# Banded attention and a gated feed-forward on one core: the planned engine order comes from four forward and backward passes instead of one

## The chip, the core and the metric

The kernel runs on one core of a Trainium2 chip. The metric is the device time of one execution in microseconds (us). The engines are named as the profile names them: PE multiplies matrices, DVE and ACT work on vectors, POOL does a little setup, and SP issues the transfers (DMA). Each engine works through its own queue of instructions in the order in which the program put them there.

## The reference, cut to what matters

```python
# q, k, v: 8 batches x 8 heads x 576 positions x 64, float32
scores = q @ k.T / sqrt(64)                     # per batch and head
mask = (rel >= 0) & (rel < 64)                  # each position sees itself and 63 before it
attn = softmax(where(mask, scores, -1e9))
x = (attn @ v), heads side by side              # 4608 tokens x 512
h = x @ w_in                                    # 512 x 2048
g = (a0 + a1*h + a2*h**2 + a3*h**3) / (1 + |b0|*|h| + |b1|*h**2 + 1e-6)
out = g @ w_out                                 # 2048 x 512, float32
```

## The kernel before, in words

**Tiles.** The 4608 tokens are cut into 12 chunks of 384 (`CH`), the 2048 hidden columns into 16 blocks of 128 (`NF`). A chunk takes four attention units (two heads each, `HP` = 4) and then 16 steps; a step is one hidden block of one chunk, so that there are 192 steps. All large products are made from split operands: each float32 operand is a high part and a low part (`xh`, `xl`; `wi_h`, `wi_l`; `gh`, `gl`; `wo_h`, `wo_l`), and three products are added up.

**A step.** `ffn1` is 12 matmuls into one of two PSUM buffers `h` (4 pieces of x, three products each). `gate` then works the rational function out: ACT squares `h`, takes |b0 h| and a3 h + a2, later a logarithm and an exponential (the division); DVE makes the rest with a multiplication by `h` and a second product with `h` (after which that buffer is free again), the denominator, `gh` and, three instructions later, `gl`. Steps 0 to 3 and the last four are gated alone, all others in pairs with tiles of 768 columns. `ffn2` is 9 matmuls into the three PSUM buffers `o` (three token tiles, three products each) and is recorded three steps after its `ffn1` (`LAG`). In the text, h8 is the `ffn1` of step 8, o8 its `ffn2`, gl 8/9 the last DVE instruction of the gate of steps 8 and 9. As two buffers `h` alternate, h8 waits for the second product with `h` of step 6.

**An attention unit.** Scores into `ps_s` (for the first three chunks the mask is put in by two matmuls from `ident_b`), the row maximum `nmx` on DVE, six exponentials on ACT with row sums `sums`, the scaling of `sm` by `rs` on DVE, transposes on PE into `ps_s`, a copy by ACT, the products with v into `ps_x`, and from these `xh` (ACT) and `xl` (DVE).

**Weights.** The 32 weight pieces come as raw 64-bit words through three staging buffers `w_st` (the first six through spare space). Each is turned into its two parts by two ACT instructions (a cast into `top`, a cast into `wi_h` or `wo_h`) and two DVE instructions (a shift, called the weight shift below, and a subtraction that gives `wi_l` or `wo_l`). The subtraction frees the staging buffer for the next fetch, which SP issues in a fixed order. The steps run in the order chunk 0 and chunk 1 with the first eight hidden blocks, then chunk 1 and chunk 0 with the other eight, then each further chunk with all 16, so that the weights are needed during steps 0 to 23.

**What sets the order.** The body of the kernel issues nothing itself. Its calls go to a `Recorder` (lines 236 to 241), which hands each to a `Planner` (line 54). That keeps them as operations with an occupancy and a latency from hand-set costs (`cost`, line 113), and works out from the tiles that they read and write which operation must follow which (`add`, line 165). `plan` (line 189) then lays all operations out on a time line of its own: again and again it takes the engine that could start next, and on that engine, among the operations that are ready, the one that was recorded first (`key=lambda o: o.index`). PE prefers one that has been ready for 300 ns (`MARGIN`). `fill` (line 217) puts warm-up matmuls into gaps that the plan leaves on PE before the first `ffn2`, and `emit` (line 229) issues everything by planned start. All instructions issued so carry the helper's line, 233 in the profile, and are told apart by their tiles. The hardware keeps each queue's order, and waits are for semaphores: an instruction that waits holds up all behind it on its engine.

Of the kernel before, what the change touches and what calls it, by code (L numbers as in the profile page):

```python
# [30 lines left out]
WARM = 7  # L31
FILL = 430
MARGIN = dict(PE=300)
C1AT = 0, 0, 1, 3
ON_PE = 2
JOIN = 4
# [17 lines left out]
class Planner:  # L54
# [58 lines left out]
    def cost(self, engine, method, out, reads, kw, args):  # L113
        if isinstance(out, Late):
            n = out.size // 4
        else:
            n = 1
            for _, k in out.ap[1:]:
                n *= k
        if engine == "SP":  # L120
            parts = 128 if isinstance(out, Late) else (out.ap[0][1] if out.tensor.__class__.__name__ != "DRamTensorHandle" else 0)
            size = mybir.dt.size(out.dtype) * n * (parts or out.ap[0][1])
            return 400, 400, size
        if engine == "PE":
            if method == "transpose":
                return 109, 270, 0
            if isinstance(args[2], Late):
                n = args[2].size // 4
            else:
                n = 1  # L130
                for _, k in args[2].ap[1:]:
                    n *= k
                if args[2].dtype == F32:
                    return (45, 270, 0) if args[1].ap[0][1] == 64 else (52, 225, 0)
            return n * 0.4545, n * 0.4545 + 165, 0
        if engine == "ACT":
            if "accum_out" in kw:
                return (343, 450, 0) if reads[0].tensor.name in self.banks else (386, 490, 0)
            f = args[2] if len(args) > 2 else None
            occ = 58 + 0.813 * n  # L140
            if n == 512:
                occ = 640 if method == "copy" and getattr(out, "dtype", None) == F16 else 510
                if reads[0].tensor.name in self.banks:
                    occ = 466
            for k in ("scale", "bias"):
                if isinstance(kw.get(k), bass.AP):
                    occ += 92
            if f in (AF.Ln, AF.Exp):
                occ += 55
            return occ, occ + 120, 0  # L150
        if engine == "DVE":
            if method == "tensor_reduce":
                n = 1
                for _, k in reads[0].ap[1:]:
                    n *= k
            if n < 16:
                return 90, 185, 0
            occ = 65 + 1.045 * n
            if isinstance(kw.get("scalar"), bass.AP):
                occ += 62  # L160
            return occ, occ + 85, 0
        if engine == "POOL":
            return (n * 2.0 + 60, n * 2.0 + 100, 0) if method in ("tensor_scalar", "tensor_copy") else (n * 2.4 + 130, n * 2.4 + 170, 0)

    def add(self, op):
        op.index, op.before, op.after = len(self.ops), set(), []
        op.ready = max([self.known.get(name, 0) for name, *_ in op.reads + op.writes], default=0)
        for is_write, spans in ((False, op.reads), (True, op.writes)):
            for name, p0, p1, b0, b1 in spans:
                for q0, q1, c0, c1, other, wrote in self.hist.get(name, ()):  # L170
                    apart = self.ops[other].engine != op.engine
                    if name in self.banks and apart or (wrote or is_write) and p0 < q1 and q0 < p1 and b0 < c1 and c0 < b1:
                        op.before.add(other)
        if op.engine == "SP":
            op.before.update(self.loads[-1:] + self.loads[-self.DMA_LANES:1 - self.DMA_LANES])
            self.loads.append(op.index)
        for other in op.before:
            self.ops[other].after.append(op)
        self.ops.append(op)
        for wrote, spans in ((False, op.reads), (True, op.writes)):  # L180
            for name, p0, p1, b0, b1 in spans:
                h = self.hist.setdefault(name, [])
                if wrote and name not in self.banks:
                    h[:] = [x for x in h if not (p0 <= x[0] and x[1] <= p1 and b0 <= x[2] and x[3] <= b1)]
                h.append((p0, p1, b0, b1, op.index, wrote))
                if name in self.shares:
                    self.hist.setdefault(self.shares[name], []).append((0, 128, 0, 1 << 20, op.index, False))

    def plan(self):
        waiting = {e: [] for e in self.free}  # L190
        missing = [len(o.before) for o in self.ops]
        for o in self.ops:
            if not o.before:
                waiting[o.engine].append(o)
        dma_free = 0
        for _ in self.ops:
            start, engine = min((max(self.free[e], min(o.ready for o in w)), e) for e, w in waiting.items() if w)
            able = [o for o in waiting[engine] if o.ready <= start]
            op = min([o for o in able if o.ready <= start - MARGIN.get(engine, 0)] or able, key=lambda o: o.index)
            waiting[engine].remove(op)  # L200
            op.start, self.free[engine] = start, start + op.occ
            op.end = start + op.own + 45
            if engine == "PE":
                op.end = self.free[engine] + 200
            if engine == "SP":
                dma_free = max(dma_free, start + 750) + op.dma / (300 if start < 8000 else 390)
                op.end = dma_free + 1550
            for o in op.after:
                o.ready = max(o.ready, self.free[engine] if engine == o.engine == "SP" and self.lanes_apart(op, o) else op.end)
                missing[o.index] -= 1  # L210
                if not missing[o.index]:
                    waiting[o.engine].append(o)

    def lanes_apart(self, op, other):
        return self.loads.index(other.index) - self.loads.index(op.index) == 1

    def fill(self, engine, name, length, call):

# [49 lines left out]
def swa_rational_ffn(ctx: ExitStack, tc: tile.TileContext, qk, v, w_in, w_out, out):  # L268
# [371 lines left out]
    for c, i0, i1 in phases:  # L640
        if c not in seen:
            seen.add(c)
            places += [(C1AT[k] if c == 1 else s - prev + prev // HP * k - AHEAD, c, k, s - prev if c > 1 else 0) for k in range(HP)]
        prev = i1 - i0
# [89 lines left out]
```

## Time and profile before

| | |
|---|---|
| time, median of 3 runs | 973.5 us (972.23 to 974.33) |
| the profiled execution's own time | 973.52 us |
| its span, first to last instruction | 971.7 us |
| PE busy | 948.9 us, 98% of the span |
| DVE busy | 856.8 us, 88% |
| ACT busy | 665.9 us, 69% |
| mean granted clock of PE | 0.995 |
| moved by DMA | 68.33 MB, 70 GB/s |

The profile is one execution. A row of its time line gives the start, the duration, the engine and the instruction with its output and inputs; in square brackets stands how long the engine sat idle before it, and what ended that. A row of its table of stages gives for each engine the busy time in that stage, then the granted clock of PE as a share of full speed. Busy times of PE are modelled at their ends: a matmul of the step is shown with 0.33 or 0.39 us, but the next one starts 0.17 or 0.23 us after it.

### The profile page before, as it was taken

The numbers are of one execution on the slowest core, as the hardware profiler recorded it, in microseconds if no ns is written. First come the engines' busy times: TensorE is split into PE (matmuls) and PEld (weight loads), VectorE is DVE, ScalarE is ACT, GpSimd is POOL, SyncE is SP. The second block draws the span as 40 slices with busy tenths as digits, with TensorE's granted clock in tenths as the row PEclk, the third lists the DMA queues.
The fourth block names the chain that finished last, engine by engine and source line by source line (L and its number), as shares of the span: only waits on it lengthen the run. The fifth ranks groups of instructions, "written<-read, shape, count | busy, mean of one in ns | idle before, by whom it ended". The sixth has DMA issues, their size and how long they took to land.

```text
span 971.7 us, 16840 instructions
## 1 busy us (share of the span) xinstructions
PE 948.9 (98%) x6673; PEld 829.1 (85%) x6673; DVE 856.8 (88%) x1287; ACT 665.9 (69%) x1553; POOL 4.4 (0%) x20
## 2 busy tenths in 40 slices
PE   8879999999999999999999999999999999999998
PEld 5667888888888888888888888888888888888896
DVE  6999998888998889888988898998889988997887
ACT  7997876766667667667666667667766766675653
POOL 1000000000000000000000000000000000000000
PEclk9998999999999999999999999999999999999999
DMA  9363431223102113112111210220211211200000
GB/s 358 117 212 109 144 128 56 80 68 101 48 22 101 35 35 101 35 35 95 41 35 67 69 35 34 68 69 12 90 35 36 101 35 36 101 1 1 33 1 32
DMA packets 24558, 68.33 MB, mean 70 GB/s; under 512 B 2720, under 2 KB 2720, under 8 KB 24480
## 3 DMA queue, kind: packets, MB, share of 16 engines
q1 hardware_dynamic: 24480, 67.27, 20.2%
q8 instruction: 52, 0.85, 0.4%
q14 instruction: 26, 0.21, 0.1%
HBM read 57.03 MB, written 10.22 MB: 69 GB/s over the span
## 4 chain that ended last, share of the span: by engine, by line
PE 88%; DVE 8%; ACT 3%; issue 1%; DMA 1%; SPq 0%; ACTq 0%; DVEq 0%
PE o L233 40%; PE h L233 38%; PE ps_s L233 6%; PE ps_x L233 4%; DVE tmp L233 3%; ACT tmp L233 1%; DVE gh L233 1%; DMA early_wi_h<-w_in 1%; DVE w_st L233 1%; DVE wi_l L233 1%; DVE gl L233 0%; DVE sm L233 0%; ACT sm L233 0%; DVE nmx L233 0%; DVE wo_l L233 0%
## 5 line engine op out<-in xcount | busy, mean ns | idle before, releaser
L233 PE MATMUL h<-xl,wi_h 128*128 128x384 f32 x768 | 260.2, 339 | 5.1 <-DVE tmp L233 4.3
L233 PE MATMUL h<-xh,wi_l 128*128 128x384 f32 x768 | 259.0, 337 | 0.0
L233 PE MATMUL h<-xh,wi_h 128*128 128x384 f32 x768 | 257.8, 336 | 0.0
L233 ACT ACTIVATE tmp<-h 128x384 f32<-128x384 f32 x192 | 94.3, 491 | 233.1 <-PE h L233 232.8
L233 PE MATMUL o<-wo_h,gl 128*128 128x512 f32 x576 | 236.4, 411 | 3.3 <-DVE gl L233 2.9
L233 PE MATMUL o<-wo_h,gh 128*128 128x512 f32 x576 | 227.7, 395 | 0.0
L233 PE MATMUL o<-wo_l,gh 128*128 128x512 f32 x576 | 227.5, 395 | 0.0
L233 ACT ACTIVATE tmp<-h,ab_sb 128x384 f32<-128x384 f32 x384 | 221.0, 629 | 2.4 <-PE h L233 2.4
L233 ACT ACTIVATE tmp<-tmp 128x768 f32<-128x768 f32 (+1 forms) x200 | 164.6, 823 | 20.6 <-DVE tmp L233 17.8
L233 PEld LDWEIGHTS h<-xl,wi_h 128*128 128x128 f32 x768 | 144.2, 188 | 16.7 <-DVE tmp L233 6.8
L233 PEld LDWEIGHTS h<-xh,wi_h 128*128 128x128 f32 x768 | 144.2, 188 | 7.4
L233 DVE SCALAR_TENSOR_TENSOR gh<-tmp,ab_sb,tmp 128x768 fp32r<-128x768 f32 (+1 forms) x100 | 98.2, 982 | 54.4 <-ACT tmp L233 54.0
L233 PEld LDWEIGHTS h<-xh,wi_l 128*128 128x128 f32 x768 | 144.1, 188 | 0.0
L233 PEld LDWEIGHTS o<-wo_h,gl 128*128 128x128 f32 x576 | 108.3, 188 | 29.0 <-issue 6.4
L233 PEld LDWEIGHTS o<-wo_h,gh 128*128 128x128 f32 x576 | 108.5, 188 | 26.6
L233 PEld LDWEIGHTS o<-wo_l,gh 128*128 128x128 f32 x576 | 108.6, 189 | 16.6
L233 DVE SCALAR_TENSOR_TENSOR tmp<-tmp,ab_sb,h 128x384 f32<-128x384 f32 x192 | 116.9, 610 | 3.0
L233 DVE SCALAR_TENSOR_TENSOR tmp<-tmp,b_sb,tmp 128x768 f32<-128x768 f32 (+1 forms) x96 | 95.8, 998 | 23.9 <-ACT tmp L233 23.8
L233 DVE TENSOR_TENSOR tmp<-tmp,h 128x384 f32<-128x384 f32 x192 | 105.1, 548 | 5.6 <-ACT tmp L233 5.4
L233 DVE SCALAR_TENSOR_TENSOR tmp<-tmp,ab_sb,tmp 128x768 f32<-128x768 f32 (+1 forms) x96 | 95.8, 998 | 1.3
L233 DVE SCALAR_TENSOR_TENSOR tmp<-tmp,gh 128x768 f32<-128x768 f32 (+1 forms) x100 | 92.1, 921 | 1.5
L233 DVE TENSOR_TENSOR gl<-tmp,tmp 128x768 fp32r<-128x768 f32 (+1 forms) x96 | 90.0, 937 | 1.5
(97 smaller groups left out, 784.4 us busy)
## 6 DMA issues: line engine op xcount, KB each, us to landing
qk<-qk SPq DMA_DIRECT2D x42, 419.0 KB, 3.3
vt<-v SPq DMA_DIRECT2D x44, 384.0 KB, 4.0
out<-ob SPq DMA_DIRECT2D x33, 256.0 KB, 2.2
w_st<-w_out SPq DMA_DIRECT2D x15, 512.0 KB, 3.7
w_st<-w_in SPq DMA_DIRECT2D x11, 512.0 KB, 3.9
early<-qk SPq DMA_DIRECT2D x6, 419.0 KB, 8.0
early<-v SPq DMA_DIRECT2D x4, 384.0 KB, 8.5
early_wi_l<-w_in SPq DMA_DIRECT2D x3, 512.0 KB, 9.4
```

Of the source, the lines that this page charges most:

```text
L233: call(*[value(x) for x in args], **{k: value(x) for k, x in kw.items()})
```

## The change

**What it does.** `plan` lays the operations out `ROUNDS` = 4 times instead of once. A round is `forward(rank)`, the old loop with one difference: among ready operations it takes the one of lowest rank. In the first round the rank is the place in the recording, as before. After each round `backward` goes through the operations from the end: it takes them in the order of their ends in the forward pass just made, keeps to the same engines, occupancies and lags, and so finds for each the time, counted back from the end, by which it must have started. Those latest times rank the next round. Of the four layouts that whose last operation ends first (by the planner's own clock) is kept. Beside this, `lag` gives one rule for the time from an operation's start to that of one that depends on it: on PE itself it is now only the occupancy (before, 200 ns more). And the cost of the large matmuls is set from n columns as 0.467 n - 6 ns instead of 0.4545 n, 0.3 ns more at 512 columns and 1.2 ns less at 384.

Nothing in the list of operations changes, nor do tiles, waits or SP's order; what changes is where an operation stands in its engine's queue, and how many warm-up matmuls `fill` adds: 30 with the seven at the start instead of 25.

```diff
+ROUNDS = 4
...
-            if isinstance(args[2], Late):
-                n = args[2].size // 4
-            else:
-                n = 1
-                for _, k in args[2].ap[1:]:
-                    n *= k
+            n = 1
+            for _, k in (args[0] if isinstance(args[2], Late) else args[2]).ap[1:]:
+                n *= k
+            if not isinstance(args[2], Late):
                 if args[2].dtype == F32:
                     return (45, 270, 0) if args[1].ap[0][1] == 64 else (52, 225, 0)
-            return n * 0.4545, n * 0.4545 + 165, 0
+            return n * 0.467 - 6, n * 0.467 + 160, 0
...
     def plan(self):
+        free, best = dict(self.free), None
+        rank = [o.index for o in self.ops]
+        for _ in range(ROUNDS):
+            self.free = dict(free)
+            length = self.forward(rank)
+            if best is None or length < best[0]:
+                best = length, [(o.start, o.end) for o in self.ops]
+            rank = self.backward()
+        for o, (o.start, o.end) in zip(self.ops, best[1]):
+            pass
+
+    def lag(self, op, other):
+        if op.engine == other.engine and (op.engine == "PE" or op.engine == "SP" and self.lanes_apart(op, other)):
+            return op.occ
+        return op.end - op.start
+
+    def forward(self, rank):
...
-            op = min([o for o in able if o.ready <= start - MARGIN.get(engine, 0)] or able, key=lambda o: o.index)
+            op = min([o for o in able if ready[o.index] <= start - MARGIN.get(engine, 0)] or able, key=lambda o: rank[o.index])
...
-                o.ready = max(o.ready, self.free[engine] if engine == o.engine == "SP" and self.lanes_apart(op, o) else op.end)
+                ready[o.index] = max(ready[o.index], start + self.lag(op, o))
...
+        return max(o.end for o in self.ops)
+
+    def backward(self):
+        waiting = {e: [] for e in self.free}
+        missing = [len(o.after) for o in self.ops]
+        free, ready, late = dict.fromkeys(self.free, 0), [0] * len(self.ops), [0] * len(self.ops)
+        for o in self.ops:
+            if not o.after:
+                waiting[o.engine].append(o)
+        for _ in self.ops:
+            time, engine = min((max(free[e], min(ready[o.index] for o in w)), e) for e, w in waiting.items() if w)
+            op = max((o for o in waiting[engine] if ready[o.index] <= time), key=lambda o: (o.start + o.occ, -o.index))
+            waiting[engine].remove(op)
+            late[op.index] = free[engine] = time + op.occ
+            for k in op.before:
+                o = self.ops[k]
+                ready[k] = max(ready[k], late[op.index] + self.lag(o, op) - o.occ)
+                missing[k] -= 1
+                if not missing[k]:
+                    waiting[o.engine].append(o)
+        return [-x for x in late]
```

**Where the order moves.** On PE the two orders differ in the first 920 of some 4300 rows (to about 225 us of the time line before) and in the last six; between them they are the same. On ACT and DVE small exchanges go on to the end. Three places follow, each of before and then of the change; line 233 of the kernel before is line 276 of the changed one.

First PE at about 67 us of the time line before, between the end of o3 (`o_74<-wo_h_136,gh_183`) and o4 (`gl_184`), where `ps_s<-ident` are a unit's transposes and `h_75<-xl_154` begins h8:

```order
L233 MATMUL o_74<-wo_h_136,gh_183 128x512
L233 MATMUL ps_s<-ident,sm_169 128x128 x6
L233 MATMUL o_72<-wo_h_136,gl_184 128x512
L233 MATMUL o_72<-wo_l_137,gh_182 128x512
L233 MATMUL o_72<-wo_h_136,gh_182 128x512
```

```order
L276 MATMUL o_74<-wo_h_136,gh_183 128x512
L276 MATMUL h_75<-xl_154,wi_h_134 128x384
L276 MATMUL h_75<-xh_150,wi_h_134 128x384
L276 MATMUL h_75<-xh_150,wi_l_135 128x384
L276 MATMUL h_75<-xl_155,wi_h_134 128x384
L276 MATMUL h_75<-xh_151,wi_h_134 128x384
L276 MATMUL h_75<-xh_151,wi_l_135 128x384
L276 MATMUL h_75<-xl_156,wi_h_134 128x384
L276 MATMUL h_75<-xh_152,wi_h_134 128x384
L276 MATMUL h_75<-xh_152,wi_l_135 128x384
L276 MATMUL o_72<-wo_h_136,gl_184 128x512
```

Nine of h8's twelve matmuls now stand ahead of the wait for gl 4/5; the transposes have gone behind six of o4's matmuls.

Then DVE at the same time, from the end of step 3's gate (`gl_185<-tmp_181`). The `w_st` rows are weight shifts and subtractions, `b_sb` marks the denominator of steps 4 and 5, and `tmp_179<-tmp_179,ab_sb,h_75` is the second product of step 6, which frees `h_75` for h8:

```order
L233 TENSOR_TENSOR gl_185<-tmp_181 128x384
L233 TENSOR_TENSOR wo_l_137<-w_st_164,wo_h_136 128x512
L233 TENSOR_TENSOR xl_156<-ps_x,xh_152 128x384
L233 SCALAR_TENSOR_TENSOR tmp_177<-tmp_177,b_sb,tmp_178 128x768
L233 SCALAR_TENSOR_TENSOR w_st_165<-w_st_165,top_138 128x512
L233 SCALAR_TENSOR_TENSOR w_st_163<-w_st_163,top_139 128x512
L233 TENSOR_REDUCE nmx_171<-ps_s 128x6
L233 TENSOR_TENSOR wo_l_137<-w_st_165,wo_h_136 128x512
L233 TENSOR_SCALAR nmx_171<-nmx_171 128x6
L233 SCALAR_TENSOR_TENSOR gh_182<-tmp_176,ab_sb,tmp_178 128x768
L233 TENSOR_TENSOR wo_l_137<-w_st_163,wo_h_136 128x512
```

```order
L276 TENSOR_TENSOR gl_185<-tmp_181 128x384
L276 SCALAR_TENSOR_TENSOR tmp_177<-tmp_177,b_sb,tmp_178 128x768
L276 TENSOR_TENSOR wo_l_137<-w_st_164,wo_h_136 128x512
L276 SCALAR_TENSOR_TENSOR w_st_165<-w_st_165,top_138 128x512
L276 TENSOR_TENSOR tmp_179<-tmp_179,h_75 128x384
L276 TENSOR_TENSOR xl_156<-ps_x,xh_152 128x384
L276 SCALAR_TENSOR_TENSOR tmp_179<-tmp_179,ab_sb,h_75 128x384
L276 SCALAR_TENSOR_TENSOR w_st_163<-w_st_163,top_139 128x512
L276 TENSOR_REDUCE nmx_171<-ps_s 128x6
L276 SCALAR_TENSOR_TENSOR gh_182<-tmp_176,ab_sb,tmp_178 128x768
```

The two products of step 6 and the denominator have moved up, weight work has moved down; the second product of step 6 stood 21 rows behind gl 3 and now stands six behind it.

Last PE's end, the final products of step 191 in the three buffers `o`:

```order
L233 MATMUL o_73<-wo_h_1005,gh_183 128x512
L233 MATMUL o_74<-wo_l_1032,gh_183 128x512
L233 MATMUL o_74<-wo_h_1005,gh_183 128x512
L233 MATMUL o_72<-wo_h_1005,gl_185 128x512
L233 MATMUL o_73<-wo_h_1005,gl_185 128x512
L233 MATMUL o_74<-wo_h_1005,gl_185 128x512
```

```order
L276 MATMUL o_73<-wo_h_1087,gh_183 128x512
L276 MATMUL o_72<-wo_h_1087,gl_185 128x512
L276 MATMUL o_74<-wo_l_1132,gh_183 128x512
L276 MATMUL o_74<-wo_h_1087,gh_183 128x512
L276 MATMUL o_73<-wo_h_1087,gl_185 128x512
L276 MATMUL o_74<-wo_h_1087,gl_185 128x512
```

The last matmul into the first buffer `o` has moved up by two.

More of the change, by code (lines that the diff above doesn't have):

```diff
@@ L166, in add @@
         op.index, op.before, op.after = len(self.ops), set(), []
-        op.ready = max([self.known.get(name, 0) for name, *_ in op.reads + op.writes], default=0)
+        op.known = max([self.known.get(name, 0) for name, *_ in op.reads + op.writes], default=0)
         for is_write, spans in ((False, op.reads), (True, op.writes)):
@@ L175, in add @@
             op.before.update(self.loads[-1:] + self.loads[-self.DMA_LANES:1 - self.DMA_LANES])
+            op.turn = len(self.loads)
             self.loads.append(op.index)
@@ L189, in plan @@
     def plan(self):
+        free, best = dict(self.free), None
[13 more added lines that the diff above has]
+    def forward(self, rank):
         waiting = {e: [] for e in self.free}
         missing = [len(o.before) for o in self.ops]
+        ready = [o.known for o in self.ops]
         for o in self.ops:
@@ L196, in plan @@
         for _ in self.ops:
-            start, engine = min((max(self.free[e], min(o.ready for o in w)), e) for e, w in waiting.items() if w)
-            able = [o for o in waiting[engine] if o.ready <= start]
-            op = min([o for o in able if o.ready <= start - MARGIN.get(engine, 0)] or able, key=lambda o: o.index)
+            start, engine = min((max(self.free[e], min(ready[o.index] for o in w)), e) for e, w in waiting.items() if w)
+            able = [o for o in waiting[engine] if ready[o.index] <= start]
+            op = min([o for o in able if ready[o.index] <= start - MARGIN.get(engine, 0)] or able, key=lambda o: rank[o.index])
             waiting[engine].remove(op)
@@ L212, in plan @@
                     waiting[o.engine].append(o)
+        return max(o.end for o in self.ops)
[18 more added lines that the diff above has]
+        return [-x for x in late]
     def lanes_apart(self, op, other):
-        return self.loads.index(other.index) - self.loads.index(op.index) == 1
+        return other.turn - op.turn == 1
     def fill(self, engine, name, length, call):
```

## The prediction

> **What bounds the kernel now.** The profiled execution took 973.52 us, which is the median of the three runs; 971.7 us is its span and 1.8 us lie outside it. I read the chain of work first, then a table of the span cut into stages.
>
> ```profile
> PE 88%; DVE 8%; ACT 3%; issue 1%; DMA 1%; SPq 0%; ACTq 0%; DVEq 0%
> ```
>
> ```profile
> core 0: us, PE busy (x) PEld busy (x) DVE busy (x) ACT busy (x) POOL busy (x), PEclk, DMA share, GB/s
> 20.00:67.00 47.00, 40.98 (x384) 32.71 (x384) 45.71 (x88) 44.70 (x112) 0.00 (x0) 1.00 0.53 183
> 67.00:73.00 6.00, 0.58 (x3) 0.47 (x3) 6.00 (x10) 5.57 (x20) 0.00 (x0) 0.88 0.63 188
> 73.00:79.00 6.00, 6.00 (x39) 4.72 (x38) 4.12 (x8) 2.19 (x4) 0.00 (x0) 0.55 0.20 76
> 79.00:123.00 44.00, 41.75 (x206) 36.28 (x205) 43.02 (x63) 36.06 (x64) 0.00 (x0) 1.00 0.40 138
> 150.00:225.00 75.00, 73.88 (x578) 63.64 (x578) 65.74 (x101) 51.34 (x132) 0.00 (x0) 1.00 0.23 76
> 225.00:944.00 719.00, 719.00 (x5020) 638.52 (x5020) 633.24 (x916) 480.76 (x1105) 0.00 (x0) 1.00 0.15 50
> ```
>
> The chain is PE's for 88%, and from 225 to 944 us PE is never idle at a full clock: no order of the same matmuls shortens that. What an order can win lies elsewhere. Until 123 us DVE is full (45.71 of 47, 6.00 of 6, 43.02 of 44 us) and PE isn't: the weights are split there, and DVE does their shifts and subtractions beside the gates. So I looked next at the time line of PE for the waits in that part.
>
> ```profile
> 66.75 0.40 PE L233 MATMUL o<-wo_h,gh 128*128 128x512 f32 x1
> ...
> 72.56 1.51 PE L233 MATMUL ps_s<-ident,sm 128*128 128x128 f32 x6 [5.42 <-DVE sm L233]
> ...
> 86.44 0.50 PE L233 MATMUL o<-wo_h,gl 128*128 128x512 f32 x1 [0.62 <-DVE gl L233]
> 96.05 0.47 PE L233 MATMUL o<-wo_h,gl 128*128 128x512 f32 x1 [0.96 <-DVE gl L233]
> 122.64 0.44 PE L233 MATMUL h<-xl,wi_h 128*128 128x384 f32 x1 [0.66 <-DVE tmp L233]
> 122.91 0.34 PE L233 MATMUL h<-xh,wi_h 128*128 128x384 f32 x1
> 123.09 0.34 PE L233 MATMUL h<-xh,wi_l 128*128 128x384 f32 x1
> ```
>
> Each wait ends on a DVE instruction, and from 25 to 150 us DVE has no pause of over 0.35 us but one, shown below. What bounds this part is therefore the amount of DVE work that stands in DVE's queue ahead of what PE needs. This is what the new order changes. The long wait has a second cost:
>
> ```profile
> 71.00:72.00 1.00, 0.00 (x0) 0.00 (x0) 1.00 (x2) 1.00 (x3) 0.00 (x0) 0.79 0.26 102
> ```
>
> ```profile
> 78.68 0.56 DVE L233 TENSOR_TENSOR xl<-ps_x,xh 128x384 fp32r<-128x384 f32 x1 [1.88 <-ACT xh L233]
> ```
>
> The granted clock of 0.79 in microsecond 71 means that it fell to one half at about 71.6, some 4.45 us after the last matmul (66.75 + 0.40); in the stage from 73 to 79 us it is 0.55 still. The slow transposes and products then leave DVE idle for 1.88 us, the one real gap in its work of this part.
>
> **What the change does to DVE's queue.** The amount of work is the same; I counted in both orders what stands ahead of each DVE result that PE waits for. The prices are distances from one start to the next:
>
> ```profile
> 81.61 0.69 DVE L233 TENSOR_TENSOR wi_l<-w_st,wi_h 128x512 fp32r<-128x512 f32 x1
> 82.22 0.95 DVE L233 SCALAR_TENSOR_TENSOR tmp<-tmp,gh 128x768 f32<-128x768 f32 x1
> 83.08 0.69 DVE L233 SCALAR_TENSOR_TENSOR w_st<-w_st,top 128x512 uint32<-128x512 uint32 x1
> ```
>
> A weight shift or subtraction costs 0.61 us (82.22 - 81.61), an instruction on 768 columns 0.86 to 0.95 (83.08 - 82.22, and its duration; I take 0.9); for one on 384 columns I take half a microsecond, a little over half of that. Ahead of the second product that frees the buffer for h18 five weight instructions and one on 768 columns have gone: 5 x 0.61 + 0.9 = 3.9 us less. Ahead of gl 18/19 it is four weight instructions less and one on 768 columns more: 1.5 us less. Ahead of gl 20/21 three weight instructions less, two on 384 columns more: 0.8 less. Ahead of gl 8/9 three less, and three gate instructions more: 0.1 more. Ahead of gl 6/7 it is 1.1 less, and ahead of gl 4/5 only 0.2.
>
> A result that comes earlier helps only as far as PE waited for it, and PE's own order moves too. How far PE may get ahead by each point is the margin there, plus DVE work gone, plus PE work that now stands ahead, plus the later waits of the part that PE then no longer has:
>
> ```profile
> 140.40 0.95 DVE L233 TENSOR_TENSOR gl<-tmp,tmp 128x768 fp32r<-128x768 f32 x1
> 147.96 0.96 DVE L233 TENSOR_TENSOR gl<-tmp,tmp 128x768 fp32r<-128x768 f32 x1
> ```
>
> ```profile
> 142.81 0.39 PE L233 MATMUL o<-wo_h,gl 128*128 128x512 f32 x1
> ...
> 149.11 0.42 PE L233 MATMUL o<-wo_h,gl 128*128 128x512 f32 x1
> ```
>
> At o18 gl 18/19 was ready 1.46 us early (142.81 - 141.35); with 1.5 less that allows 2.9. At o20 the margin was 0.19; with 0.8 less, and a whole h (12 matmuls, about 2.0 us) newly ahead of o20, 3.0. At o8 the matmuls placed ahead bring 2.0, and the wait of 0.66 at h18 goes: 2.7 less 0.1. At o6, 1.1 gained, and 0.96 and 0.66 that come later: 2.7. I take **-2.7 us** by about 150 us; what is late next is gl 8/9.
>
> **The wait at o4.** Nine of h8's matmuls now stand between o3 and the wait.
>
> ```profile
> 72.33 0.95 DVE L233 TENSOR_TENSOR gl<-tmp,tmp 128x768 fp32r<-128x768 f32 x1
> ```
>
> The second product of step 6, for which h8 waits, stood behind this row; in the new queue it stands some 9 us of DVE work earlier, so h8 can begin when o3 ends, at 67.15. Matmuls of an h follow each other by 0.18 us (123.09 - 122.91), so nine take 1.6, and the whole twelve of the term above about 2.1. gl 4/5 was ready at 73.28 and comes 0.2 us earlier, so PE pauses for 73.08 - 67.15 - 1.6 = 4.3 us instead of 5.42. The 1.0 us won is not added: the 2.7 above counts how far PE may be ahead in the end. The clock fell 4.45 us after the idle began, so a pause of 4.3 us stands on the edge. If the clock still drops, the slow stretch holds other work and DVE's gap shrinks little: -0.5. If it holds, the whole gap of 1.88 goes: -1.9. I take the middle, **-1.2 us**.
>
> [...]
>
> **Warm-ups.** Five more are issued, two places early in the program. The costs:
>
> ```profile
> 29.34 1.68 PE L233 MATMUL o<-warm 128*128 128x512 bf16 x7
> 32.66 0.44 PE L233 MATMUL h<-xl,wi_h 128*128 128x384 f32 x1 [1.64 <-DVE tmp L233]
> ...
> 40.18 0.44 PE L233 MATMUL h<-xl,wi_h 128*128 128x384 f32 x1 [1.48 <-DVE tmp L233]
> ```
>
> One is 1.68 / 7 = 0.24 us, five are 1.2. PE waits for DVE right behind them by 1.64 and 1.48 us, which hides them: nothing, and +1.2 if that cover were gone.
>
> **From 150 to 225 us.** By the table of stages DVE has 75.00 - 65.74 = 9.3 us of idle time here and PE 75.00 - 73.88 = 1.1, 0.47 of it in one wait. The orders still differ.
>
> ```profile
> 222.97 0.45 PE L233 MATMUL h<-xl,wi_h 128*128 128x384 f32 x1 [0.47 <-DVE tmp L233]
> ```
>
> ```profile
> DVE gh L233 <- ACT tmp L233: 4.7, 5, 1.7
> ```
>
> DVE idles behind ACT's parts of the gate, which wait for PE; a PE that is ahead lets that idle time shrink. But PE has to stay ahead: the new queue has 2.3 us more DVE work ahead of gl 24/25 (a row maximum, one product on 384 and one on 768 columns), 0.9 more ahead of the product that frees the buffer for h30, 0.5 more ahead of gl 34/35, and 1.3 us of PE work less ahead of h30. Against 2.7 + 1.2 won that gives back between nothing (the idle time absorbs it) and all of 3.9. The 2.3 is the largest single one, but two more matmul groups (2.0 us) stand ahead of o22 and o24 as well, which leaves 0.3 there; behind it 0.9 + 1.3 = 2.2 at h30 less a margin I can't read. I take a third of the whole, **+1.4 us**.
>
> **The end.**
>
> ```profile
> 966.35 0.86 PE L233 MATMUL o<-wo_h,gl 128*128 128x512 f32 x3
> 966.78 1.07 ACT L233 COPY w_st<-o 128x512 f32<-128x512 f32 x2 [5.18 <-PE o L233]
> 967.39 1.31 SPq L233 DMA_DIRECT2D out<-w_st  x3
> ```
>
> The last three matmuls end one output buffer each, and SP issues the three stores one after another, 1.31 / 3 = 0.44 us each. In the new order the first buffer ends two matmuls (0.47 us) earlier, so its copy and the first store do too, and the chain of three begins earlier. **-0.3 us**, between 0 and -0.5, as the last copy does not move.
>
> **The sum.** -2.7 - 1.2 + 1.4 - 0.3 = -2.8, and 973.5 - 2.8 = **970.7 us**. About 0.2% (1.95 us) is what a measurement of this kernel tells from no change: below 971.55 is faster, above 975.45 slower.
>
> **The rivals.**
>
> *Given back.* The DVE work ahead of gl 24/25, h30 and gl 34/35 takes all that was won; only the end's 0.3 stays: 973.2 us. For it: this part has waits already, 1.1 us, and what PE is ahead at 150 us it must still be ahead at 225. Against it: 9.3 us of DVE idle time. Chance 0.20.
>
> *The clock holds, and nothing is given back.* 973.5 - 2.7 - 1.9 - 0.3 = 968.6. It needs the pause before o4 on the good side of the edge and DVE's idle time to be as elastic as it looks. Chance 0.14.
>
> *A staging buffer comes back too late (slower).* A subtraction frees a `w_st`, SP fetches, ACT casts, and the next shift of that buffer follows on DVE.
>
> ```profile
> w_st<-w_out SPq DMA_DIRECT2D x15, 512.0 KB, 3.7
> ```
>
> ```profile
> ACT top L233 <- DMA w_st<-w_out: 2.4, 3, 1.2
> ```
>
> ```profile
> L233 ACT CAST top<-w_st 128x512 f16<-128x512 bf16 x26 | 20.4, 794 | 3.2 <-DMA w_st<-w_out 2.4 <-DMA w_st<-w_in 0.8
> ```
>
> In the old queue at least 6.3 us of DVE work (by the prices above) stand between a subtraction and the next shift of its buffer; in the new one four times only 5.0 to 5.8. [...] ACT already waits 2.4 us for such fetches in three places, 1.2 us the longest. With a little more than that, 1.3 us, lost at each of the four, 5.2 less the 2.8 of the sum: +2.4, **975.9 us**. Against it: only three of 15 such fetches were waited for. Chance 0.14.
>
> That the change does nothing is left out: the two orders differ where PE waits.
>
> **How the numbers follow.** The forecast has 0.52, with 968.8 to 972.3 as its own range (-2.7 - 1.7 - 0.3 with the clock nearly held and nothing given back; -2.7 - 0.5 + 2.3 - 0.3 with it dropped and more given back): 0.45 of it faster, 0.07 within 0.2%. It is the likeliest since its first two terms rest on counts and rows, and only the third is a choice. With the clock that holds, faster is 0.45 + 0.14, and 0.01 of the second rival comes to it: 0.60. Within 0.2%: 0.07 + 0.19 = 0.26. Slower: 0.14. The range of 8 in 10 reaches from 968.2, a little below the third case, to 974.6, above the second and below the staging case.
>
> **What would show it.** In the profile after: a wait of about 4.3 us before o4 (5.42 before), the granted clock of one half shorter or gone; the gap of 1.88 before `xl` smaller; no wait at h18 and o20 about 3 us earlier in the time line; PE idle from 150 to 225 us of 1.1 us and up to 1.4 more; ACT's waits for `w_st<-w_out` near 2.4 us; the first store 0.4 us earlier against the last matmul. Wrong would be: ACT or DVE waiting over 6 us for `w_st`, h8 waiting at PE's head for step 6 behind a late product, or PE idle time of over 2 us between 150 and 225 us.

## The result, and the profile after

The changed kernel takes 967.71 us, the median of six runs (966.55 to 969.24); the kernel before, timed beside it, 973.46 us. The ratio is 0.9943 with a 95% interval from 0.9933 to 0.9954: faster by 5.75 us, twice what was forecast and just outside the range. The profiled execution took 968.40 us, 5.1 us less than that of before, and all that follows about its parts explains these 5.1.

The chain of waits and the table of stages of the changed kernel, cut as before:

```profile
PE 85%; DVE 6%; ACT 5%; DMA 2%; issue 1%; SPq 0%; ACTq 0%
```

```profile
0.00:20.00 20.00, 16.26 (x186) 9.70 (x187) 11.87 (x31) 12.65 (x54) 4.35 (x20) 0.91 0.91 346
...
67.00:73.00 6.00, 2.55 (x14) 2.06 (x12) 6.00 (x11) 5.15 (x19) 0.00 (x0) 0.94 0.28 91
73.00:79.00 6.00, 5.46 (x16) 4.49 (x17) 5.08 (x8) 3.07 (x5) 0.00 (x0) 0.50 0.41 126
79.00:123.00 44.00, 43.62 (x237) 38.24 (x236) 42.72 (x63) 34.95 (x63) 0.00 (x0) 1.00 0.37 121
...
150.00:225.00 75.00, 74.80 (x600) 64.72 (x600) 67.73 (x106) 52.79 (x135) 0.00 (x0) 1.00 0.26 88
```

DVE is as full as it was until 123 us; PE is busier beside it (43.62 of 44 us instead of 41.75). From 150 to 225 us PE's idle time has gone from 1.1 to 0.2 us, where the forecast had it grow. The granted clock is one half from 73 to 79 us, as it nearly was before (0.55), and there is a new dip in the first 20 us (0.91; 1.00 before). Two waits of the kernel before that were not shown yet, and then PE's waits in the changed kernel, those that answer to waits of before and others:

```profile
191.88 0.50 PE L233 MATMUL o<-wo_h,gl 128*128 128x512 f32 x1 [0.24 <-DVE gl L233]
...
214.59 0.50 PE L233 MATMUL o<-wo_h,gl 128*128 128x512 f32 x1 [0.39 <-DVE ob L233]
```

```profile
10.97 0.80 PE L276 MATMUL ps_s<-mask,ident_b 128*128 128x384 bf16 x2 [2.62 <-ACT sm L276]
...
73.55 0.79 PE L276 MATMUL o<-wo_h,gl 128*128 128x512 f32 x1 [3.99 <-DVE gl L276]
...
94.17 0.44 PE L276 MATMUL h<-xl,wi_h 128*128 128x384 f32 x1 [0.38 <-DVE tmp L276]
...
139.30 0.89 PE L276 MATMUL ps_s<-qk 64*64 64x128 f32 x24 [0.57 <-DMA qk<-qk]
...
171.44 0.50 PE L276 MATMUL o<-wo_h,gl 128*128 128x512 f32 x1 [0.20 <-DVE gl L276]
```

The wait before o4 is 3.99 us, near the 4.3 foretold, and the waits of 0.62 (o6), 0.96 (o8), 0.66 (h18), 0.24 (o28), 0.39 (o32) and 0.47 us (h38) are gone; there are new ones of 0.38 (h12), 0.57 and 0.20 us (o24). The gap on DVE behind the half clock is not:

```profile
79.14 0.69 DVE L276 TENSOR_TENSOR wi_l<-w_st,wi_h 128x512 fp32r<-128x512 f32 x1 [1.05 <-ACT wi_h L276]
...
81.25 0.56 DVE L276 TENSOR_TENSOR xl<-ps_x,xh 128x384 fp32r<-128x384 f32 x1 [0.55 <-ACT xh L276]
```

1.05 + 0.55 = 1.60 us stand where 1.88 stood. To see where the time went, take the lead: by how much the same matmul starts earlier than in the profiled execution of before. Up to each of these points PE has done the same matmuls in all kernels, added warm-ups aside, so that the lead changes only by waits, clock and order. There is one exception: with the ranks on PE alone, PE has already done six matmuls of an `ffn2` at h20 that the others do behind it. Those are worth 6 x 0.233 = 1.4 us, so that at equal work this kernel's lead at h20 is 1.5 us.

| kernel | median, us | lead at h4 | h20 | h41 | last step's h | end of the span | half clock (us of that profile) |
|---|---|---|---|---|---|---|---|
| changed | 967.71 | -0.70 | 3.05 | 4.41 | 4.77 | 5.12 | 10.9 to 14.3, 72.3 to 79.1 |
| one round | 971.41 | 0.62 | 2.41 | 2.48 | 2.45 | 2.44 | none |
| old costs | 970.75 | -2.00 | -0.03 | 1.35 | 1.71 | 1.71 | 12.0, 35.9 (3.4 each), 73.4 to 80.3 |
| ranks on PE | 971.83 | 0.45 | 0.07 (1.5 at equal work) | 2.06 | 2.03 | 2.35 | 71.5 to 75.0 |
| ranks on the rest | 970.52 | -0.39 | 4.08 | 2.51 | 2.84 | 2.84 | 11.7 to 15.1, 73.1 to 79.9 |
| ranks up to step 20 | 973.22 | -0.15 | 4.77 | 0.67 | 0.66 | 0.66 | 11.2, 72.7, 137.5 (3.4 each) |
| ranks from step 20 | 968.42 | 1.35 | 3.14 | 5.49 | 5.85 | 6.18 | none |
| warm-ups before o4 | 965.72 | 0.76 | 6.10 | 7.77 | 8.13 | 8.47 | none |
| warm-ups early | 965.63 | 1.03 | 5.52 | 7.19 | 7.55 | 7.89 | 72.2 to 75.6 |
| both | 965.06 | 0.23 | 5.80 | 7.40 | 7.76 | 8.10 | none |
| old end | 968.57 (one run) | 0.27 | 3.72 | 4.98 | 4.95 | 4.95 | 71.7 to 78.5 |
| before, warm-ups | 973.03 | -0.47 | 0.16 | 0.08 | 0.04 | 0.04 | 12.0, 73.5 (3.4 each) |

The first row shows the changed kernel's 5.1 us: 0.70 lost up to h4, 3.75 won from there to h20 (at 128 us), 1.36 from h20 to h41, nothing in the 700 us behind it, 0.36 just before the last step and 0.35 at the very end. (The kernel before has the half clock from 71.6 to 78.4 us, and 3.4 us of it cost some 0.9 us, as shown below; a row with 3.4 us of it there, or none, owes some 0.9 or 1.8 us of its lead to that. The half clock at the very end, from 969.3 us on in the profile of before and behind PE's last matmul, is left out. The lead at h4 also holds how long PE was slow at the start of that execution: the first two matmuls on `mask` took 0.80 us in the profile of before, from 4.24 us on, and 0.49 in the changed kernel's, from 4.23.)

### The profile page after: what moved, and what is told of

It is laid out like the page before. It is cut to its first block, busy times and chain, and to the rows that moved or that the text cites. A ratio compares the mean times of both kernels' runs of the same rounds, so it can differ in the third digit from the quotient of the medians.

```text
span 966.6 us, 16862 instructions
## 1 busy us (share of the span) xinstructions
PE 948.1 (98%) x6678; PEld 830.8 (86%) x6678; DVE 853.6 (88%) x1287; ACT 666.8 (69%) x1553; POOL 4.4 (0%) x20
## 4 chain that ended last, share of the span: by engine, by line
PE 85%; DVE 6%; ACT 5%; DMA 2%; issue 1%; SPq 0%; ACTq 0%
PE o L276 39%; PE h L276 37%; PE ps_s L276 6%; PE ps_x L276 4%; DVE tmp L276 4%; ACT tmp L276 2%; ACT sm L276 1%; ACT top L276 1%; DVE gl L276 1%; DVE w_st L276 1%; DMA early_wi_h<-w_in 1%; DVE gh L276 1%; DMA qk<-qk 1%; DMA w_st<-w_out 1%; ACT wi_h L276 0%
## 5 line engine op out<-in xcount | busy, mean ns | idle before, releaser
L276 ACT ACTIVATE tmp<-tmp 128x768 f32<-128x768 f32 (+1 forms) x200 | 164.8, 824 | 15.1 <-DVE tmp L276 11.6
L276 ACT ACTIVATE sm<-sm,nmx 128x128 f32<-128x128 f32 x216 | 83.6, 391 | 16.1 <-DVE nmx L276 16.1
```

Source lines behind the costliest of these rows:

```text
L276: call(*[value(x) for x in args], **{k: value(x) for k, x in kw.items()})
```

## The experiments

Each kernel is an edit of the changed kernel, but for one, an edit of the kernel before, and all were timed in alternation with the kernel before, but for the one with the old end, which ran once. My theory after the result: the two costs' edits matter little; the ranks shorten two separate stretches by two separate means, and the half clock is a cost beside them that the change doesn't touch. Rivals: the costs do it all; the later stretch only keeps what the first one wins; the half clock is hidden behind DVE.

**One round, and old costs.**

```diff
-ROUNDS = 4
+ROUNDS = 1
```

> One layout only, in the recorded order, with the new lag and the new cost of the matmuls. If the gain comes from the ranks that the backward passes give (first theory), this is within 1 us of the kernel before, 972.5 to 974.5 us, with the 5 us pause of PE near 67 us still in it. If it comes from the two edits of the planner's costs alone (rival), it is near the changed kernel, 967 to 969 us.

971.41 us, ratio 0.9990 [0.9981, 0.9999]. And the reverse, four rounds with the lag and the matmul cost of before:

```diff
-            return n * 0.467 - 6, n * 0.467 + 160, 0
+            return n * 0.4545, n * 0.4545 + 165, 0
...
-        if op.engine == other.engine and (op.engine == "PE" or op.engine == "SP" and self.lanes_apart(op, other)):
+        if op.engine == other.engine == "SP" and self.lanes_apart(op, other):
```

> Four layouts with the ranks from behind, but with the lag and the matmul cost of the kernel before. First theory: most of the gain stays, 967 to 970 us. Rival (costs): 972 to 974 us.

970.75 us, ratio 0.9969 [0.9961, 0.9978], a little above what was expected. Neither alone gives the 0.9943, so both expectations failed in part: the rounds are worth more, but with the old costs the lead at h20 is nil. Of that, 2.0 us are lost by h4, where its profile has two stretches of the half clock; from h4 on it gains 2.0 us up to h20 and 1.4 to h41. Two of its 11 runs have a mean clock of 0.995, as two of the changed kernel do: 967.92 and 969.09 us against 968.40 and 968.81. So what the old costs lose may be mostly the clock of the first 43 us; no run separates that.

In the one-round kernel the pause of 5 us, which was expected to stay, is not there. Two waits have taken its place, before h8 and o6:

```profile
68.48 0.44 PE L276 MATMUL h<-xl,wi_h 128*128 128x384 f32 x1 [1.97 <-DVE tmp L276]
...
81.76 0.50 PE L276 MATMUL o<-wo_h,gl 128*128 128x512 f32 x1 [2.05 <-DVE gl L276]
```

Six of its 11 runs took 971.0 to 971.4 us, the others 972.4 to 974.6, and the profiled one, of 971.08, has no half clock before the end. From h4 to h20 it gains 1.8 us, about what the half clock costs the kernel before, as shown below. Its waits behind h20 are those of before:

```profile
189.44 0.50 PE L276 MATMUL o<-wo_h,gl 128*128 128x512 f32 x1 [0.24 <-DVE gl L276]
...
212.16 0.50 PE L276 MATMUL o<-wo_h,gl 128*128 128x512 f32 x1 [0.39 <-DVE ob L276]
...
220.54 0.44 PE L276 MATMUL h<-xl,wi_h 128*128 128x384 f32 x1 [0.49 <-DVE tmp L276]
```

**Ranks on one side only.** After the rounds one more layout is made, with the best round's ranks on some engines and the recorded order on the others.

```diff
-                best = length, [(o.start, o.end) for o in self.ops]
+                best = length, rank
...
+        rank = [r if o.engine == "PE" else o.index for o, r in zip(self.ops, best[1])]
+        self.free = dict(free)
+        best = self.forward(rank), [(o.start, o.end) for o in self.ops]
```

> The latest times rank PE alone; DVE, ACT and SP take what was recorded first, as before. If it is the amount of DVE work ahead of what PE waits for (the prediction's theory), PE's order alone wins little: 971.5 to 973.5 us. If it is PE that fills its own waits with other matmuls (rival), most of the gain is here: 968 to 970 us.

971.83 us, ratio 0.9989 [0.9980, 0.9998]. The reverse exchanges the two cases of the first line:

> The latest times rank DVE, ACT and SP; PE takes what was recorded first. DVE theory: most of the gain is here, 968 to 970.5 us. PE theory: 971.5 to 974 us. If it takes both engines together, this and the PE-only kernel both stay above 971 us.

970.52 us, ratio 0.9968 [0.9956, 0.9981], just above the band for DVE's theory. The medians alone would say "mostly DVE"; the leads say more. With the ranks on DVE, ACT and SP the lead at h20 is 4.08 us, more than in the changed kernel, and 1.6 of it is lost again by h41, where PE runs in the old order into a wait of 1.65 us:

```profile
201.40 0.84 PE L279 MATMUL ps_s<-ident,sm 128*128 128x128 f32 x6 [0.38 <-DVE sm L279]
...
224.00 0.50 PE L279 MATMUL o<-wo_h,gl 128*128 128x512 f32 x1 [1.65 <-DVE gl L279]
```

The second is o34, which waits for gl 34/35. With the ranks on PE alone and equal work, 1.0 us is won from h4 to h20, some 0.9 of which is the half clock, 3.4 us shorter; from h20 to h41 it is 0.6 us (2.06 less 1.47). So up to 130 us it is the order on DVE and ACT, as the prediction argued. From there to 240 us neither side does it alone: PE's ranks win 0.6, the others' lose 1.6, and both together win 1.4 in the changed kernel and 2.3 in one below.

**Ranks in one stretch only.** The same added layout, split by the place in the recording (operations up to step 20 or behind it):

```diff
...
+        rank = [(0, r) if o.index < self.split else (1, o.index) for o, r in zip(self.ops, best[1])]
...
+        if s == 20:
+            pl.split = len(pl.ops)
```

> Operations recorded up to step 20 are ranked by the latest times, the later ones by the recording. If what was won up to 130 us stays to the end without the later exchanges, the lead over the kernel before is about 3 us from there on: 969.5 to 971 us. If the old order behind it gives the lead back (the second rival of the prediction), 972 to 973.5 us.

973.22 us, ratio 1.0000 [0.9991, 1.0009]: all of a lead of 4.77 us at h20 is lost but 0.66. This is the prediction's rival "given back", but not by DVE work. PE's and SP's rows there:

```profile
136.82 0.96 PE L279 MATMUL ps_s<-qk 64*64 64x128 f32 x24 [1.90 <-DMA qk<-qk]
...
148.48 0.47 PE L279 MATMUL o<-wo_h,gl 128*128 128x512 f32 x1 [0.62 <-DVE sums L279]
```

```profile
117.96 13.44 SPq L279 DMA_DIRECT2D w_st<-w_out  x5
131.46 0.42 SPq L279 DMA_DIRECT2D qk<-qk  x1
```

The recorded order puts the third chunk's first scores at the old place, while its load `qk` stands in SP's queue behind the last weight fetches, each of which needs a staging buffer that a subtraction on DVE has freed. As the new order has put weight work back on DVE, the load is issued later than in the kernel before:

```profile
128.52 1.38 SPq L233 DMA_DIRECT2D qk<-qk  x1
```

That is 2.9 us (131.46 - 128.52), while PE comes to the scores 4.8 us earlier; it waits for 1.90 us, and the granted clock is one half from 137.50 to 140.91 us. In the changed kernel the scores stand later; the row at 139.30 above shows what is left of this wait, 0.57.

```diff
+        rank = [(0, o.index) if o.index < self.split else (1, r) for o, r in zip(self.ops, best[1])]
```

> The reverse: recorded order up to step 20, latest times behind it. The first part is then near the one-layout kernel, 971.4 us; if the later exchanges are worth the 1.4 us by which the changed kernel's lead grows between 131 and 225 us and 0.7 us at the end, this is 1.5 to 2 us less, 969 to 970 us. If they only work behind the new first part, 971 to 973 us.

968.42 us, ratio 0.9956 [0.9943, 0.9968], better than expected. From h20 to h41 the three kernels compare as follows, before, one round, and ranks from step 20 (the columns are those of the table of stages):

```profile
131.20:241.70 110.50, 109.26 (x811) 94.12 (x810) 98.09 (x148) 75.66 (x192) 0.00 (x0) 1.00 0.25 82
```

```profile
128.70:239.20 110.50, 109.24 (x812) 94.22 (x811) 98.18 (x148) 75.75 (x192) 0.00 (x0) 1.00 0.24 81
```

```profile
128.00:236.20 108.20, 108.20 (x811) 94.47 (x811) 96.10 (x148) 74.96 (x191) 0.00 (x0) 1.00 0.25 83
```

The same 811 matmuls take 108.2 us with no idle time at all, instead of 110.5 with 1.24. The idle time shown is not all that these waits cost: in the profile of before the matmul after each of the three starts about 0.15 us later than idle time alone says (0.40 for 0.24, 0.55 for 0.39, 0.63 for 0.47, against the usual distance of the same two matmuls). From start to start the three cost 1.6 us; what makes up the rest of the 2.3 was not traced. So the later ranks win 2.3 us by themselves behind h20 and another 0.7 at the end.

**The half clock.** Two edits that put warm-up matmuls into pauses; no other instruction changes its place. The first writes them to `ps_x` ahead of the products of the second chunk's last unit:

```diff
+        if (c, hp) == (1, 3):
+            for _ in range(14):
+                pl.tensor.matmul(ps_x, *warm_up[1:], start=True, stop=True)
```

> The changed kernel with 14 warm-up matmuls into the buffer ps_x, 9 of them in the 4 us pause before o4 and 5 ahead of it among the matmuls of h8 and o3; all else stands in the same order. If the half clock from 72 to 79 us costs time (the prediction's clock term), it is away in every run and the time falls by 1.5 to 2.5 us, to 965.3 to 966.3 us. If DVE's queue sets that part anyway (rival), no change or up to 0.5 us more, from the warm-ups that don't fit: 967.5 to 968.2 us.

965.72 us, ratio 0.9926 [0.9913, 0.9938]. Seven of the 14 stand together in the pause (nine were expected), and the wait left before o4 is 0.84 us:

```profile
69.56 1.68 PE L276 MATMUL ps_x<-warm 128*128 128x512 bf16 x7
72.08 0.50 PE L276 MATMUL o<-wo_h,gl 128*128 128x512 f32 x1 [0.84 <-DVE gl L276]
```

The second lets `fill` reckon with 240 ns for a warm-up up to 11 us, instead of 430:

```diff
+            length = 240 if time < 11000 else FILL
             while time + length <= following.start and following.start <= until:
```

> The changed kernel with 15 instead of 8 warm-up matmuls in the pause before the second unit's scores (8.4 to 11 us). If the half clock at 10.9 to 14.3 us, which some runs show, is what separates runs at 966.6 from runs at 968.8 us, all runs come near the lower end, median 966.5 us, with a spread under 1.5 us. If the early part is not on the path, median and spread stay, 967.7 us from 966.5 to 969.3.

965.63 us, ratio 0.9925 [0.9914, 0.9937], 965.09 to 967.06: a better median than expected, but a spread of 2.0 us where under 1.5 was expected. Its three runs near 965.4 show a clock of 0.998 (one stretch of 3.4 us at half clock in that profile), the two near 966.9 one of 0.996. Then both edits together:

> The changed kernel with both sets of warm-ups, in the early pause and in the one before o4; the rest in the same order. If both half clocks cost time by themselves, no run shows one and the time is that of the best runs with either, 964.5 to 965.3 us, with a spread under 1 us. If the two costs are the same cost (the later part of DVE's queue takes up what is won early), it stays at 965.6 to 965.8 us.

965.06 us, ratio 0.9915 [0.9902, 0.9929], all five runs from 964.66 to 965.44 us with a mean clock of 0.999 or 1.0; the profiled one has no half clock before the end. This is the fastest version, 2.65 us under the changed kernel's median, and most of that kernel's spread of 2.7 us is gone. The leads give the price: from h4 to h20, with one order, 3.75 (changed) and 3.45 us (old end) are won with 6.8 us of the half clock, 4.49 with 3.4 us of it (early warm-ups), and 5.34 and 5.57 without (warm-ups before o4, both). So 3.4 us at half clock cost some 0.9 us here. For the kernel before, whose order stays what it was:

> The kernel before, its order unchanged, with the same 14 warm-ups into ps_x, 11 of them in its 5.42 us pause. If the half clock behind the pause costs it what the prediction said (DVE's gap of 1.88 us goes), 970.8 to 971.8 us. If DVE's queue sets that part anyway, 972.6 to 973.5 us.

973.03 us, ratio 0.9993 [0.9985, 1.0002], no difference in the median; but the edit didn't do what it was to do. Warm-ups fill 2.55 us of the pause, 2.45 remain, and in seven of 11 runs the mean clock was still 0.995 to 0.998:

```profile
68.05 2.55 PE L233 MATMUL ps_x<-warm 128*128 128x512 bf16 x11
73.05 1.12 PE L233 MATMUL ps_s<-ident,sm 128*128 128x128 f32 x6 [2.45 <-DVE sm L233]
```

The four runs with a mean clock of 1.0 took 971.33 to 971.61 us, the five with 0.996 973.03 to 973.69: some 1.9 us. In the profiled one, of 0.996, that is for two stretches of 3.4 us, of which one lies behind the pause and the other at 12 us, so this is no measure of the pause alone.

**The old end.** As above, with the split at step 180, ranks ahead of it and the recorded order behind.

> The changed kernel with the operations recorded from step 180 on ranked as before; on PE only the last six rows differ from it. If the exchanges at the end are worth what the traces show, 0.36 us before the last step and 0.35 us behind it, the stretch from step 150 to the end is 0.7 us longer than in the changed kernel, as in the kernel before. The prediction's end term says 0.3 us.

From step 150 to the end the lead goes from 4.98 to 4.95, against 4.41 to 5.12 in the changed kernel: the exchanges at the end are worth 0.7 us, as expected. Half of it is a wait before h190, which costs 0.25 us from start to start, and 0.11 us more up to h191, which DVE's new order removes (with the ranks on the rest: 2.50 to 2.84), half the stores behind PE's last rows (with the ranks on PE: 2.03 to 2.35). In the changed kernel these read:

```profile
961.54 0.58 ACT L276 COPY w_st<-o 128x512 f32<-128x512 f32 x1 [4.73 <-PE o L276]
...
961.81 0.63 PE L276 MATMUL o<-wo_h,gl 128*128 128x512 f32 x2
962.15 1.62 SPq L276 DMA_DIRECT2D out<-w_st  x3
```

## Why the prediction was wrong

By its own terms, for the profiled execution:

| term | foretold, us | measured, us |
|---|---|---|
| up to h4 (warm-ups "nothing") | 0 | +0.70 |
| DVE's queue and the clock, h4 to h20 | -2.7 - 1.2 = -3.9 | -3.75 |
| 150 to 225 us, given back (measured from h20 to h41, 128 to 237 us) | +1.4 | -1.36 |
| the end | -0.3 | -0.71 |
| sum | -2.8 | -5.12 |

**The step that failed is the one from 150 to 225 us**: 2.8 us between its term and the measured one, more than the whole miss of 2.3 us in this execution. It foretold that lead would be given back, and more was won. It counted what DVE has to do ahead of gl 24/25, h30 and gl 34/35, priced each, and took a third of what could be lost; it set PE's own order against this at two places and gave up on the third ("less a margin I can't read"). Its counts of DVE's work hold, and where PE keeps the recorded order, lead is given back, 1.6 us with the ranks on the rest, at o34 behind the gl 34/35 that it had named; that this is near its 1.4 is luck, as the third was a choice. What it had wrong is PE's order. It counted that only as matmuls that stand ahead of a wait, and not as what lets a gate begin. With the ranks on PE h35 stands ahead of the nine matmuls of an `ffn2` that the recorded order puts before it, and so gl 34/35 is done earlier. The first `ffn1` matmuls of h34 and h35, gl 34/35 and o34 with the ranks on the rest, and then in the changed kernel:

```profile
202.79 0.34 PE L279 MATMUL h<-xl,wi_h 128*128 128x384 f32 x1
208.84 0.34 PE L279 MATMUL h<-xl,wi_h 128*128 128x384 f32 x1
222.99 0.95 DVE L279 TENSOR_TENSOR gl<-tmp,tmp 128x768 fp32r<-128x768 f32 x1
224.00 0.50 PE L279 MATMUL o<-wo_h,gl 128*128 128x512 f32 x1 [1.65 <-DVE gl L279]
```

```profile
203.44 0.34 PE L276 MATMUL h<-xl,wi_h 128*128 128x384 f32 x1
207.29 0.44 PE L276 MATMUL h<-xl,wi_h 128*128 128x384 f32 x1
220.90 0.95 DVE L276 TENSOR_TENSOR gl<-tmp,tmp 128x768 fp32r<-128x768 f32 x1
222.20 0.39 PE L276 MATMUL o<-wo_h,gl 128*128 128x512 f32 x1
```

h35 comes 3.9 us behind h34 instead of 6.1 (6.1 in the kernel before too), and PE has no wait at o34. The whole stretch wins 1.4 us in the changed kernel, and with both sides' ranks from step 20 it has no idle time left. The waits of 1.1 us that I had quoted as there already were the price of the old order, and I never asked whether the change removes them. All of the lead was given back in one kernel, the one with the old order behind step 20, but by a load that stood behind weight fetches on SP's queue, a wait that the prediction did not name.

**The first stretch came out right as a sum, and wrong in its parts.** The clock still fell, for the same 6.83 us, and DVE's gap behind it shrank by 0.28: the clock term of -1.2 measures nothing to -0.3. So what the order won there is some 3.5 us, where the term said 2.7: the term counted the lead at four points and took 2.7, near the smallest, while of the 2.24 us that PE waited behind o4 only 0.38 is left. That it was DVE's and ACT's order that mattered there is shown (from h4 to h20 4.5 us are won with the ranks on the rest, and 1.0 with those on PE, nearly all of it by the clock).

**The clock's edge was no edge.** The prediction read "4.45 us after the idle began" as a time that a pause must reach, and put the new pause of 4.3 on the limit. The clock fell 2.8 us after the idle began in the changed kernel (69.56 to 72.32). The 4.45 us held for that one execution. The prediction took the middle between a fall and none; the clock fell in both profiles of this order without the added warm-ups in the pause that were taken (here and in the kernel with the old end), and in the one with early warm-ups.

**The warm-ups were not all free of charge, but not as costs on PE.** PE's waits behind the five more shrank to 1.50 and 0.95 us and hid them. What was lost is 0.7 us by h4, with a half clock from 10.9 to 14.3 us. It comes in some runs only, and early warm-ups remove it: the six runs of the changed kernel fall into 966.55 to 967.02 us with a mean clock of 0.996 to 0.997, and 968.40 to 969.24 with 0.994 to 0.995, and the profiled one is of the second kind. The median of 967.71 lies between the two, which is why it is 0.7 us better than the profile and fell below the range, in which the profiled 968.40 still lies.

**The rivals.** ACT's waits for staging buffers did grow, over the 6 us that the prediction called a sign of trouble:

```profile
L276 ACT CAST top<-w_st 128x512 f16<-128x512 bf16 x26 | 20.1, 793 | 6.3 <-DMA w_st<-w_in 3.2 <-DMA w_st<-w_out 3.0
```

That is 3.1 us more than before, and it cost next to nothing: 10.4 us of such waits stand in the kernel with the ranks on the rest, beside a lead of 4.08 us at h20. The sign was badly chosen: in the changed kernel's profile no shift in a staging buffer made DVE wait over 0.15 us for its cast. In the profile of before SP mostly issues a fetch 0.03 us after the subtraction ends, the median fetch takes 3.7 us, and where ACT waited, its cast of 0.79 us starts 0.02 to 0.08 us after the landing: some 4.6 us in all, against the 5.0 to 5.8 us of DVE work that the prediction counted.

The end was right in kind, and mis-sized: its stores gave 0.35, as foretold; the wait before the last step had not been seen, since its idle time (0.08 us) was too small to look at.

## What to carry to other kernels

Count a new order on both sides of a wait: the work queued ahead of the result and the start of what the result is made from, and the work that its reader now has to do first; where one side can't be read, give the term no sign. A wait in the old profile inside a stretch that the change reorders is a gain to be priced, not a sign of more waits to come. Pauses of 2.6 and 4 us on PE in front of a dense part were worth filling with matmuls that nothing needs (967.71 to 965.06 us with both), though another engine seemed to set the time. When two kernels are compared at the same instruction, check that the engine has done the same work up to there.

## What the runs showed of the hardware

The granted clock was one half for 3.41 us (10.88 to 14.29) and for 6.83 us (72.32 to 79.15) in the profile of the changed kernel, and for 6.83 us (71.58 to 78.41) in that of before; in the table of leads the stretches are of about 3.4 and 6.8 us. Three stretches of 3.41 us and what came after each, read from the table of stages (behind the length stands PE's busy time; the granted clock is third from the end), of the changed kernel, the one with ranks on the rest, and the one with ranks from step 20:

```profile
68.90:72.32 3.42, 0.65 (x4) 0.33 (x2) 3.42 (x6) 2.90 (x14) 0.00 (x0) 1.00 0.47 153
72.32:79.15 6.83, 5.61 (x16) 4.64 (x17) 5.78 (x11) 3.52 (x5) 0.00 (x0) 0.50 0.38 119
```

```profile
8.26:11.67 3.41, 1.62 (x28) 0.84 (x26) 1.97 (x5) 3.41 (x22) 0.00 (x0) 1.00 1.02 403
11.67:15.08 3.41, 3.19 (x32) 2.47 (x32) 2.96 (x7) 3.24 (x16) 0.00 (x0) 0.50 1.04 415
```

```profile
66.01:69.42 3.41, 1.67 (x9) 1.51 (x9) 3.41 (x7) 3.41 (x10) 0.00 (x0) 1.00 0.00 0
69.42:72.83 3.41, 3.29 (x37) 2.44 (x36) 3.41 (x7) 1.62 (x3) 0.00 (x0) 1.00 0.20 56
```

In the changed kernel 3.42 us with PE busy for 0.65 (19%) were followed by the half clock; in the kernel with the ranks on the rest so were 3.41 us with 1.62 (47%); in the kernel with the ranks from step 20, 3.41 us with 1.67 (49%) were not. The length of a wait alone did not tell the two outcomes apart: the wait of 1.90 us before 136.82 in the kernel with ranks up to step 20 was followed by the half clock from 137.50 us on, and one of 1.98 us before 67.75 in the kernel with ranks from step 20 was not. What does decide was not shown, and no run was made to find how long a pause may be. Runs of the same kernel differ by 1.6 to 3.9 us, and by 0.8 us with both pauses filled, where the mean clock of every run is 0.999 or 1.0.
